# Grouped attention on one core: reordering the first loads, moving ScalarE's skip branch, and respacing the final range test

## The chip, the core and the metric

The kernel runs on one core of a Trainium2 chip. The core has five engines that run their own instruction streams and meet at semaphores: TensorE (PE, with its weight loads listed as PEld), VectorE (DVE), ScalarE (ACT), GpSimd (POOL) and SyncE (SP), which here issues every transfer. The metric is the device time of one execution in microseconds (us), lower is better. Three runs of the kernel before took 540.35, 540.84 and 541.56 us, median 540.84.

## The reference

The inputs are q (16 batches, 32 heads, 288 rows, 128 columns) and k and v (16 batches, 8 heads, 512 rows, 128 columns), all bf16 normals times 0.05. Four query heads share one key and value head.

```python
k = jnp.repeat(k, rep, axis=1)
v = jnp.repeat(v, rep, axis=1)
scale = D ** -0.5
scores = jnp.einsum("bhqd,bhkd->bhqk", q, k) * scale
p = _softmax(scores, axis=-1)
return jnp.einsum("bhqk,bhkd->bhqd", p, v)
```

## The kernel before

**Groups, slots, units.** A group is one key/value head of one batch with its 4 x 288 = 1152 query rows, which are 9 tiles of 128 rows. There are 128 groups, numbered g. The scores of one group, keys on the partitions, are 4 x 1152 = 4608 columns; they are cut into NC = 3 slots of 1536 columns, so there are 384 slots, numbered n. Four groups make a unit u; k and v are loaded by unit into NSLOT = 3 buffers, q by group into NQ = 12 buffers, and the output is stored by group from NO = 6 buffers.

**One slot.** PE computes the scores of slot n (`op_s`, L499) into one of two score buffers. ACT takes exp of them (`op_exp`, L537) with no maximum subtracted. PE multiplies with v, for the three row tiles of slot n - 4 (`op_pv`, L519; LAG = 4): 12 matmuls of 129 columns, where the 129th column of v is ones and gives the row sum. The output lies in one of two PSUM banks. DVE takes the reciprocals of the three row sums (`op_rc`, L554) and multiplies them into the output (`op_ev`, L565). In the text the product, the reciprocal and the multiplication of slot r are called pv(r), rc(r) and ev(r). POOL copies v to where the column of ones stands (`op_vc`, L547).

**What a step waits for.** The scores of slot n wait for k and q of the group and for the exp of slot n - 2. pv(r) waits for ev(r - 2), since it writes the same bank. ev(r) of a group g of 6 or more waits, on DVE and ahead of everything behind it there, until the store of group g - 6 has landed, since both use the same output buffer:

```python
waits = [("s_rc", r + 1)]
if g >= NO:
    waits.insert(0, ("s_o%d" % (g % NO), 16 * (g // NO)))
```

So ev(18), the first of group 6, waits for store 0; ev(24), the first of group 8, for store 2.

**SP's order.** SP issues all transfers in one stream: first the list `first` (k of groups 0 to 3 one by one, q of groups 0 to 3, v of groups 0 to 3), then the list `sp`, sorted by a due time written for each transfer (L600 to L611). k and q are transposing transfers (L432 and L453), v (L444) and the stores (L467, and L472 for the three pieces of the last group) are plain. Before the change the list opens with: q of groups 4, 5, 6, 7, then k of unit 1, q 8, v of unit 1, q 9, q 10, q 11, k of unit 2, v of unit 2, q 12, q 13, store 0, q 14, store 1, q 15, store 2, k of unit 3, v of unit 3, q 16, store 3.

**The fallback and the flag.** Since no maximum is subtracted, the kernel keeps a second, general program for inputs whose row sums leave a range. A flag chooses it at the end. DVE reduces all reciprocals to their largest and smallest (`op_stat`, L582 and L584, once per batch, and L669 and L671 over the batches) and compares them with the limits (`op_over`, L589 and L592). The reciprocals of the last ALONE = 15 row tiles (5 slots) are compared one by one, behind the last reciprocal. PE adds the comparisons over the partitions (L631), DVE adds the rest to one number (L674), and every engine loads it (L373) and branches on it (L377). SP, ahead of its branch, waits there until all stores have landed. All engines then drain and meet at a barrier (L329).

**Where the general code lies.** Each engine's instructions of the general program lie somewhere in its stream, and the function `general` makes it branch past them (L362). For POOL, DVE and SP this is near the top; for ACT it is between the last slot and the flag; for PE the code lies behind the end.

Of the kernel before, what the change touches and what calls it, by code (L numbers as in the profile page):

```python
# [287 lines left out]
def bass_standalone__gqa_softmax__near_ridge_kernel(  # L288
# [5 lines left out]
):  # L294
    B, Hq, Sq, D = q.shape
    _, Hkv, Sk, _ = k.shape
    P = 128
    R = (Hq // Hkv) * Sq
    NJ = Sk // P
    NT = R // P  # L300
    G = Hkv
    NG = B * G
    assert D == P and Sk % P == 0 and R % P == 0
    BANK = 512
    TPC = 3
    CH = TPC * BANK
    COLS = NJ * R
    NC = COLS // CH
# [3 lines left out]
    LAG = NC + 1  # L312
    UG = 4
    NU = NG // UG
    NSLOT = 3
    NQ = 12
    NPT = 3
    NO = 6
    NS = NG * NC
    LASTG = NG - 1  # L320
    ALONE = 5 * TPC


    q_v = q.rearrange("b h s d -> (b h s) d").rearrange("(x t) d -> x (t d)", t=NT)
# [4 lines left out]
    with ExitStack() as es:  # L329
# [29 lines left out]
        def general(eng, key, after):  # L359

            home[key] = nc.cur_bb
            eng.br(after + key)  # L362
            with nc.body("general_" + key):
                if key == "sp":
                    eng.sem_inc(sem["s_go"], 1)
                fns[key](eng)
                eng.br("done_" + key)
            nc.switch_bb(after + key)
# [25 lines left out]
        rl_sb = main.enter_context(nc.sbuf_tensor("rl_sb", [P, NG * NT], FP32))  # L394
        st_sb = main.enter_context(nc.sbuf_tensor("st_sb", [P, 2, B], FP32))
        ck_sb = main.enter_context(nc.sbuf_tensor("ck_sb", [P, 3], FP32))
        bad_sb = main.enter_context(nc.sbuf_tensor("bad_sb", [P, 2, ALONE + 1], FP32))
        one_f = main.enter_context(nc.sbuf_tensor("one_f", [P, 1], FP32))
# [6 lines left out]
        def need(eng, waits):  # L405

            left = []
            for (s, n) in waits:
                key = (id(eng), s)
                if seen.get(key, 0) < n:  # L410
                    seen[key] = n
                    left.append((sem[s], n))
            return left

        def emit(eng, waits, fn):
            waits = need(eng, waits)
            for (s, n) in waits[:-1]:
                eng.wait_ge(s, n)
            ins = fn()
            if waits:  # L420
                ins.wait_op(waits[-1][0], waits[-1][1], "sem-ge")
            return ins


        def op_k(u, gi=None):
            eng = nc.sync
            sl = u % NSLOT
            if u >= NSLOT:
                for (s, n) in need(eng, [("s_s", NC * UG * (u - NSLOT + 1))]):
                    eng.wait_ge(s, n)  # L430
            g0, g1 = (0, UG) if gi is None else (gi, gi + 1)
            eng.dma_start_transpose(  # L432
                kt_sb[:, sl, :, g0:g1].rearrange("d j g p -> d j (g p)"),
                k_v[(u * UG + g0) * P:(u * UG + g1) * P]
            ).then_inc(sem["us_k%d" % sl if gi is None else "s_k%d" % gi], 16)

        def op_v(u, gi=None):
            eng = nc.sync
            sl = u % NSLOT
            if u >= NSLOT:  # L440
                for (s, n) in need(eng, [("s_vc", UG * (u - NSLOT + 1))]):
                    eng.wait_ge(s, n)
            g0, g1 = (0, UG) if gi is None else (gi, gi + 1)
            eng.dma_start(  # L444
                vd_sb[:, sl, g0:g1], v_v[:, u * UG + g0:u * UG + g1]
            ).then_inc(sem["us_v%d" % sl if gi is None else "s_v%d" % gi], 16)

        def op_q(g):
            eng = nc.sync
            if g >= NQ:  # L450
                for (s, n) in need(eng, [("s_s", NC * (g - NQ + 1))]):
                    eng.wait_ge(s, n)
            eng.dma_start_transpose(qt_sb[:, g % NQ], q_v[g * P:(g + 1) * P]).then_inc(sem["s_q%d" % (g % NQ)], 16)  # L453
# [71 lines left out]
        def op_exp(n):  # L525
            eng = nc.scalar
            g, i = n // NC, n % NC
            waits = [("s_s", n + 1)]
            if g >= NPT:
                waits.insert(0, ("s_pv", NC * (g - NPT + 1)))  # L530
            if g == LASTG:
                w = TPC * P
                dst = pt_sb[:, g % NPT].rearrange("p (j r) -> p j r", r=R)[:, :, i * w:(i + 1) * w]
                src = ps_s[:, n % 2].rearrange("p (j r) -> p j r", r=w)
            else:
                dst, src = pt_sb[:, g % NPT, i * CH:(i + 1) * CH], ps_s[:, n % 2]
            emit(eng, waits, lambda: eng.activation(dst, src, ACTF.Exp, scale=scale)).then_inc(sem["s_e"], 1)  # L537
# [40 lines left out]
        def op_stat(b):  # L578
            eng = nc.vector
            w = G * NT  # L580
            a, e = b * w, (b + 1) * w - (ALONE if b == B - 1 else 0)
            emit(eng, [("s_rc", e // TPC)], lambda: eng.tensor_reduce(  # L582
                st_sb[:, 0, b:b + 1], rl_sb[:, a:e], AX.X, ALU.max))
            eng.tensor_reduce(st_sb[:, 1, b:b + 1], rl_sb[:, a:e], AX.X, ALU.min).then_inc(sem["s_stat"], 1)  # L584

        def op_over(hi, lo, x0, x1, wait, n):

            eng = nc.vector
            emit(eng, [wait], lambda: eng.tensor_scalar(  # L589
                out=bad_sb[:, 0, x0:x1], in0=hi, scalar1=SUM_MAX, scalar2=None, op0=ALU.is_gt)  # L590
            ).then_inc(sem["s_stat"], 1)
            emit(eng, [("s_stat", n)], lambda: eng.scalar_tensor_tensor(  # L592
                out=bad_sb[:, 1, x0:x1], in0=lo, scalar=1.0 / SUM_MAX, in1=bad_sb[:, 0, x0:x1],
                op0=ALU.is_lt, op1=ALU.add)).then_inc(sem["s_bad"], 1)
# [2 lines left out]
        first = [lambda: op_k(0, 0), lambda: op_q(0), lambda: op_k(0, 1), lambda: op_q(1), lambda: op_v(0, 0)]  # L597
        first += [lambda: op_k(0, 2), lambda: op_q(2), lambda: op_v(0, 1)]
        first += [lambda: op_k(0, 3), lambda: op_q(3), lambda: op_v(0, 2), lambda: op_v(0, 3)]
        sp = []  # L600
        for u in range(1, NU):
            t = -1.0 + u if u < NSLOT else NC * UG * (u - NSLOT + 1) + LAG
            sp.append((t, lambda u=u: op_k(u)))
            sp.append((t + 0.2, lambda u=u: op_v(u)))
        for g in range(UG, NG):
            sp.append((-0.9 + g / UG - 1.0 if g < NQ else NC * (g - NQ + 1) + 1.2, lambda g=g: op_q(g)))
        for g in range(LASTG):
            sp.append((NC * (g + 1) + LAG + 1.5, lambda g=g: op_store(g)))
        for i in range(NC):
# [3 lines left out]
        @block.sync  # L613
        def _(eng):
            for fn in first:
                fn()
            general(eng, "sp", "main_")
            for (_, fn) in sp:
                fn()
            choose(eng, "sp")  # L620

        @block.tensor
        def _(eng):
            for n in range(NS + LAG):
# [6 lines left out]
            emit(eng, [("s_ev", NS - 1), ("s_bad", 2)], lambda: eng.matmul(  # L631
                ps_o[0:1, NS % 2, 0:ALONE + 1], one_f[:], bad_sb[:, 1, :], start=True, stop=True)
            ).then_inc(sem["s_bad"], 1)
            choose(eng, "pe", behind=True)

        @block.scalar
        def _(eng):
            emit(eng, [("s_one", 1)], lambda: eng.activation(dum[:, 1:2], dum[:, 0:1], ACTF.Exp))  # L638
            for n in range(NS):
                op_exp(n)  # L640
            op_ev_last()
            general(eng, "act", "end_")
            choose(eng, "act")

        @block.gpsimd
# [7 lines left out]
        @block.vector  # L653
        def _(eng):
            eng.memset(dum[:], 0.0).then_inc(sem["s_one"], 1)  # L655
            eng.memset(one_f[:], 1.0)
            general(eng, "dve", "main_")
            per_b = G * NC
            for r in range(NS):
                op_rc(r)  # L660
                if r == NS - 1:
                    last = rl_sb[:, NG * NT - ALONE:NG * NT]
                    op_over(last, last, 0, ALONE, ("s_rc", NS), B + 3)
                op_ev(r)
                if r % per_b == per_b - 1 and r < NS - 1:
                    op_stat(r // per_b)
                if r == NS - 1 - ALONE // TPC:
                    op_stat(B - 1)
                    emit(eng, [("s_stat", B)], lambda: eng.tensor_reduce(  # L669
                        ck_sb[:, 0:1], st_sb[:, 0, :], AX.X, ALU.max))  # L670
                    eng.tensor_reduce(ck_sb[:, 1:2], st_sb[:, 1, :], AX.X, ALU.min).then_inc(sem["s_stat"], 1)  # L671
                    op_over(ck_sb[:, 0:1], ck_sb[:, 1:2], ALONE, ALONE + 1, ("s_stat", B + 1), B + 2)
            with nc.allow_low_precision(reason="a count of at most 2048"):
                emit(eng, [("s_bad", 3)], lambda: eng.tensor_reduce(  # L674
                    flag_i[:], ps_o[0:1, NS % 2, 0:ALONE + 1], AX.X, ALU.add)).then_inc(sem["s_flag"], 1)
            choose(eng, "dve")
# [30 lines left out]
```

## Time and profile before

| what | value |
|---|---|
| median of three runs | 540.84 us |
| the profiled execution | 541.11 us |
| its span in the profile | 539.4 us |
| outside the span | 1.71 us |
| PE busy in the span | 524.0 us (97%) |
| ACT busy | 522.1 us (97%) |
| DVE busy | 288.5 us (53%) |
| POOL busy | 73.8 us (14%) |
| transfers, mean | 204 GB/s, 110.08 MB |

The span is counted from the first instruction to the last one that the profile shows; times inside it are given from its start. A row of the timeline gives start, length, engine, line, operation, and in brackets how long the engine was idle before and for what. A row of the view of one line gives count, shortest, median and longest duration in ns, and first and last start. SP's rows are the issues of transfers; how long after the start of its issue a transfer has landed is a row of its own. The granted clock (PEclk) is the share of TensorE's full clock in a stretch.

### The profile page before, as it was taken

The numbers are of one execution on the slowest core, as the hardware profiler recorded it, in microseconds if no ns is written. First come the engines' busy times: TensorE is split into PE (matmuls) and PEld (weight loads), VectorE is DVE, ScalarE is ACT, GpSimd is POOL, SyncE is SP. The second block draws the span as 40 slices with busy tenths as digits, with TensorE's granted clock in tenths as the row PEclk, the third lists the DMA queues.
The fourth block names the chain that finished last, engine by engine and source line by source line (L and its number), as shares of the span: only waits on it lengthen the run. The fifth ranks groups of instructions, "written<-read, shape, count | busy, mean of one in ns | idle before, by whom it ended". The sixth has DMA issues, their size and how long they took to land.

```text
span 539.4 us, 14538 instructions
## 1 busy us (share of the span) xinstructions
PE 524.0 (97%) x6152; PEld 411.2 (76%) x6152; DVE 288.5 (53%) x809; ACT 522.1 (97%) x387; POOL 73.8 (14%) x133
## 2 busy tenths in 40 slices
PE   4799999999999999999999999999999999999997
PEld 1577777777777777777777777777777777777776
DVE  0445555555555555555555555555555555555555
ACT  5889999999999999999999999999999999999995
POOL 1021211100111101111101111101111101111000
PEclk9989999999999999999999999999999999999999
DMA  6999999999899988899998999989899988995212
GB/s 133 178 216 246 281 247 292 260 203 190 219 212 228 207 209 219 192 215 232 205 183 220 219 215 233 211 186 199 224 220 225 219 182 216 204 224 154 87 67 92
DMA packets 253944, 110.08 MB, mean 204 GB/s; under 512 B 220848, under 2 KB 237616, under 8 KB 253872
## 3 DMA queue, kind: packets, MB, share of 16 engines
q1 hardware_dynamic: 253872, 109.08, 90.2%
q8 instruction: 50, 0.82, 0.6%
q14 instruction: 22, 0.18, 0.1%
HBM read 16.78 MB, written 37.75 MB: 101 GB/s over the span
## 4 chain that ended last, share of the span: by engine, by line
PE 94%; ACT 3%; DVE 1%; DMA 1%; issue 1%; SPq 0%
PE ps_o L519 49%; PE ps_s L499 45%; ACT pt_sb L537 3%; DMA qt_sb<-in_q_dram 1%; DVE o_sb L565 0%; SPq L432 0%; DVE rl_sb L554 0%; DVE bad_sb L589 0%; DVE bad_sb L592 0%; DVE ck_sb L669 0%; DVE st_sb L584 0%; DVE flag_i L674 0%; DVE st_sb L582 0%; DVE ck_sb L671 0%
## 5 line engine op out<-in xcount | busy, mean ns | idle before, releaser
L537 ACT ACTIVATE pt_sb<-ps_s 128x1536 bf16<-128x1536 f32 x384 | 520.2, 1452 | 10.6 <-PE ps_s L499 10.6
L519 PEld LDWEIGHTS ps_o<-v_sb,pt_sb 128*128 128x128 bf16 x4596 | 300.2, 98 | 55.0 <-DVE o_sb L565 0.6
L519 PE MATMUL ps_o<-v_sb,pt_sb 128*128 128x129 bf16 x4596 | 332.6, 221 | 0.4 <-DVE o_sb L565 0.4
L499 PE MATMUL ps_s<-qt_sb,kt_sb 128*128 128x512 bf16 (+3 forms) x1542 | 313.8, 326 | 11.6 <-DMA qt_sb<-in_q_dram 6.7
L565 DVE TENSOR_TENSOR o_sb<-ps_o,rl_sb 128x384 bf16<-128x384 f32 x383 | 213.6, 558 | 13.5 <-DVE rl_sb L554 0.3
L554 DVE RECIPROCAL rl_sb<-ps_o 128x3 f32<-128x3 f32 x383 | 69.3, 181 | 233.9 <-PE ps_o L519 233.9
L499 PEld LDWEIGHTS ps_s<-qt_sb,kt_sb 128*128 128x128 bf16 x1542 | 130.2, 98 | 69.5 <-DMA qt_sb<-in_q_dram 6.7
L547 POOL COPY v_sb<-vd_sb 128x512 bf16<-128x512 bf16 x128 | 73.3, 616 | 421.3 <-DMA vd_sb<-in_v_dram 392.5
L584 DVE TENSOR_REDUCE st_sb<-rl_sb 128x1 f32<-128x72 f32 (+1 forms) x16 | 3.5, 217 | 0.0
L582 DVE TENSOR_REDUCE st_sb<-rl_sb 128x1 f32<-128x72 f32 (+1 forms) x16 | 3.5, 217 | 0.0
L573 ACT ACTIVATE o_sb<-ps_s,rl_sb 128x128 bf16<-128x128 f32 x1 | 0.4, 368 | 2.9 <-DVE rl_sb L554 2.9
L638 ACT ACT_TABLE_LOAD x1 | 1.3, 1283 | 0.8 <-PEq L692 0.8
L631 PE MATMUL ps_o<-bad_sb,one_f 128*1 128x16 f32 x2 | 0.2, 176 | 0.7 <-DVE bad_sb L592 0.7
L519 PE MATMUL ps_s<-v_sb,pt_sb 128*128 128x129 bf16 x12 | 0.9, 221 | 0.0
L631 PEld LDWEIGHTS ps_o<-bad_sb,one_f 128*1 128x1 f32 x2 | 0.1, 80 | 0.9 <-DVE bad_sb L592 0.9
L519 PEld LDWEIGHTS ps_s<-v_sb,pt_sb 128*128 128x128 bf16 x12 | 0.7, 98 | 0.0
L655 DVE MEMSET dum<- 128x2 f32 x1 | 0.1, 60 | 0.9 <-PEq L692 0.9
L565 DVE TENSOR_TENSOR o_sb<-ps_s,rl_sb 128x256 bf16<-128x256 f32 x1 | 0.4, 418 | 0.0
L647 POOL MEMSET v_sb<- 128x48 bf16 x1 | 0.3, 311 | 0.3 <-POOLq L692 0.3
L638 ACT ACTIVATE dum<-dum 128x1 f32<-128x1 f32 x1 | 0.2, 203 | 0.0
L592 DVE SCALAR_TENSOR_TENSOR bad_sb<-rl_sb,bad_sb 128x15 f32<-128x15 f32 x1 | 0.2, 175 | 0.0
L589 DVE TENSOR_SCALAR bad_sb<-rl_sb 128x15 f32<-128x15 f32 x1 | 0.2, 174 | 0.0
(11 smaller groups left out, 1.4 us busy)
## 6 DMA issues: line engine op xcount, KB each, us to landing
out_dram<-o_sb SPq DMA_DIRECT2D x127, 288.0 KB, 3.4
vd_sb<-in_v_dram SPq DMA_DIRECT2D x31, 512.0 KB, 5.1
qt_sb<-in_q_dram SPq DMA_TRANSPOSE x128, 4.6
kt_sb<-in_k_dram SPq DMA_TRANSPOSE x35, 4.7
vd_sb<-in_v_dram SPq DMA_DIRECT2D x4, 128.0 KB, 2.9
out_dram<-o_sb SPq DMA_DIRECT2D x3, 96.0 KB, 1.8
```

The costliest lines, as they stand in the source:

```text
L499: ins = emit(eng, waits if x == 0 else [], lambda: eng.matmul(ps_s[:, n % 2, c:c + w], kt_sb[:, sl, j, gi, :], qg[:, r0:r0 + w], start=Tru ...
L519: ins = emit(eng, waits if a == 0 and j == 0 else [], lambda: eng.matmul(outs(r)[:, a, :], pt_sb[:, g % NPT, j * R + t * P:j * R + (t + 1) ...
L537: emit(eng, waits, lambda: eng.activation(dst, src, ACTF.Exp, scale=scale)).then_inc(sem["s_e"], 1)
L547: emit(eng, waits, lambda: eng.tensor_copy(v_sb[:, sl, gi * NJ:(gi + 1) * NJ, 0:D], vd_sb[:, sl, gi].rearrange("p (j d) -> p j d", d=D))). ...
L554: emit(eng, [("s_pv", r + 1)], lambda: eng.reciprocal(rl_sb[:, TPC * r:TPC * (r + 1)].unsqueeze(2), outs(r)[:, :, D:DV])).then_inc(sem["s_ ...
L565: emit(eng, waits, lambda: eng.tensor_tensor(out=o_sb[:, g % NO, t0:t0 + n, :], in0=outs(r)[:, 0:n, 0:D], in1=rl_sb[:, TPC * r:TPC * r + n ...
L573: emit(eng, [("s_o%d" % (LASTG % NO), 16 * (LASTG // NO)), ("s_rc", NS)], lambda: eng.activation(o_sb[:, LASTG % NO, NT - 1, :], outs(NS - ...
L582: emit(eng, [("s_rc", e // TPC)], lambda: eng.tensor_reduce(st_sb[:, 0, b:b + 1], rl_sb[:, a:e], AX.X, ALU.max))
L584: eng.tensor_reduce(st_sb[:, 1, b:b + 1], rl_sb[:, a:e], AX.X, ALU.min).then_inc(sem["s_stat"], 1)
L631: emit(eng, [("s_ev", NS - 1), ("s_bad", 2)], lambda: eng.matmul(ps_o[0:1, NS % 2, 0:ALONE + 1], one_f[:], bad_sb[:, 1, :], start=True, st ...
L638: emit(eng, [("s_one", 1)], lambda: eng.activation(dum[:, 1:2], dum[:, 0:1], ACTF.Exp))
L647: eng.memset(v_sb[:, :, :, D:DV], 1.0)
```

## The change

It has three parts.

1. In SP's list the transfers ahead of the first slots are reordered: k of unit 1, q 4, q 5, v of unit 1, q 6, q 7, k of unit 2, q 8, q 9, v of unit 2, q 10, q 11, then q 12, q 13, store 0 as before. From unit 3 on, k is due at the first slot of a unit plus 0.5 where it was due 4 slots later, and v stays due 4 slots behind it. After store 0 the list reads q 14, store 1, k of unit 3, q 15, store 2, v of unit 3, q 16, store 3.
2. ACT branches past its general code right behind its first small activation, and not behind its last one.
3. ALONE becomes 24 (8 slots). The reductions over the batches and their comparison, which followed one another behind ev(378), stand behind ev(375), ev(376) and ev(377). The comparison of the last 24 reciprocals, which stood between rc(383) and ev(383), stands behind ev(383).

```diff
-    ALONE = 5 * TPC
+    ALONE = 8 * TPC
...
         for u in range(1, NU):
-            t = -1.0 + u if u < NSLOT else NC * UG * (u - NSLOT + 1) + LAG
-            sp.append((t, lambda u=u: op_k(u)))
-            sp.append((t + 0.2, lambda u=u: op_v(u)))
+            t = NC * UG * (u - NSLOT + 1) if u >= NSLOT else -2 * NC * UG + u
+            sp.append((t + 0.5, lambda u=u: op_k(u)))
+            sp.append((t + (LAG if u >= NSLOT else 0.65), lambda u=u: op_v(u)))
         for g in range(UG, NG):
-            sp.append((-0.9 + g / UG - 1.0 if g < NQ else NC * (g - NQ + 1) + 1.2, lambda g=g: op_q(g)))
+            t = NC * (g - NQ + 1) + 1.2 if g >= NQ else -2 * NC * UG + g // UG + 0.51 + 0.1 * (g % UG)
+            sp.append((t, lambda g=g: op_q(g)))
...
             emit(eng, [("s_one", 1)], lambda: eng.activation(dum[:, 1:2], dum[:, 0:1], ACTF.Exp))
+            general(eng, "act", "main_")
             for n in range(NS):
                 op_exp(n)
             op_ev_last()
-            general(eng, "act", "end_")
             choose(eng, "act")
...
             per_b = G * NC
+            w0 = NS - 1 - ALONE // TPC
+            last = rl_sb[:, NG * NT - ALONE:NG * NT]
             for r in range(NS):
                 op_rc(r)
-                if r == NS - 1:
-                    last = rl_sb[:, NG * NT - ALONE:NG * NT]
-                    op_over(last, last, 0, ALONE, ("s_rc", NS), B + 3)
                 op_ev(r)
                 if r % per_b == per_b - 1 and r < NS - 1:
                     op_stat(r // per_b)
-                if r == NS - 1 - ALONE // TPC:
+                if r == w0:
                     op_stat(B - 1)
+                if r == w0 + 1:
                     emit(eng, [("s_stat", B)], lambda: eng.tensor_reduce(
                         ck_sb[:, 0:1], st_sb[:, 0, :], AX.X, ALU.max))
                     eng.tensor_reduce(ck_sb[:, 1:2], st_sb[:, 1, :], AX.X, ALU.min).then_inc(sem["s_stat"], 1)
+                if r == w0 + 2:
                     op_over(ck_sb[:, 0:1], ck_sb[:, 1:2], ALONE, ALONE + 1, ("s_stat", B + 1), B + 2)
+            op_over(last, last, 0, ALONE, ("s_rc", NS), B + 3)
```

## The prediction

> **What bounds the kernel now.** The page first, for the size of things; then ScalarE's timeline over the whole span, because a kernel with two engines at 97% loses time only where both stop.
>
> ```profile
> span 539.4 us, 14538 instructions
> DMA  6999999999899988899998999989899988995212
> out_dram<-o_sb SPq DMA_DIRECT2D x127, 288.0 KB, 3.4
> kt_sb<-in_k_dram SPq DMA_TRANSPOSE x35, 4.7
> ```
>
> ```profile
> 8.18 16.22 ACT L537 ACTIVATE pt_sb<-ps_s 128x1536 bf16<-128x1536 f32 x12 [5.88 <-PE ps_s L499]
> 28.46 1.45 ACT L537 ACTIVATE pt_sb<-ps_s 128x1536 bf16<-128x1536 f32 x1 [4.06 <-PE ps_s L499]
> 30.62 502.54 ACT L537 ACTIVATE pt_sb<-ps_s 128x1536 bf16<-128x1536 f32 x371 [0.71 <-PE ps_s L499]
> 536.01 0.37 ACT L573 ACTIVATE o_sb<-ps_s,rl_sb 128x128 bf16<-128x128 f32 x1 [2.85 <-DVE rl_sb L554]
> ```
>
> From 30.62 us on, 371 exps run without a gap at 502.54 / 371 = 1.355 us each: the pace of a slot. No part of the change touches that pace. What it can touch is the hole between the 12th and 14th exp (4.06 + 0.71 us) and the tail behind the last exp. PE's timeline and the stretches around the hole show what it is:
>
> ```profile
> 22.50 0.87 PE L519 MATMUL ps_o<-v_sb,pt_sb 128*128 128x129 bf16 x12
> 26.99 1.44 PE L499 MATMUL ps_s<-qt_sb,kt_sb 128*128 128x512 bf16 x4 [3.63 <-issue]
> ```
>
> ```profile
> 23.40:26.60 3.20, 0.00 (x0) 0.00 (x0) 0.74 (x2) 1.00 (x1) 0.00 (x0) 1.00 1.03 203
> 26.60:30.00 3.40, 3.01 (x18) 2.04 (x19) 0.20 (x2) 1.45 (x1) 0.00 (x0) 0.50 1.17 235
> ```
>
> PE runs pv(7) at 22.50 and then stands idle for 3.63 us until the scores of slot 12, the first of unit 1. When it resumes its granted clock (third number from the end) is 0.50 until about 30.0. What it waited for is in SP's timeline:
>
> ```profile
> 14.36 7.66 SPq L453 DMA_TRANSPOSE qt_sb<-in_q_dram  x4
> 22.05 2.15 SPq L432 DMA_TRANSPOSE kt_sb<-in_k_dram  x1
> 25.86 0.58 SPq L444 DMA_DIRECT2D vd_sb<-in_v_dram  x1
> 40.01 0.58 SPq L467 DMA_DIRECT2D out_dram<-o_sb  x1
> 44.07 0.57 SPq L467 DMA_DIRECT2D out_dram<-o_sb  x1
> 44.68 2.69 SPq L432 DMA_TRANSPOSE kt_sb<-in_k_dram  x1
> ```
>
> k of unit 1 is issued at 22.05, behind four q transfers that are needed later; with the median 4.7 us to landing it is there at 26.75, and PE starts at 26.99. That is the stall part 1 aims at.
>
> **Part 1, the hole, and where the stall goes.** In the new order k of unit 1 is issued at 14.36 and q 4 behind it. The scores of slot 12 would want them about 0.7 us behind the start of pv(7), at 23.2. k issued at 14.36 lands near 14.36 + 4.7 = 19.1; q 4 follows at the pace 7.66 / 4 = 1.92 us of an issue, near 21. Both are in time, so this wait goes. The next transfers too: q 5 and v 1 follow within some 5 us and are wanted three slots (4.1 us) and four slots later.
>
> What is late next? The stores. The row of the multiplications up to ev(18), the issue-to-landing of store 0, and two rows of the timeline there:
>
> ```profile
> L565 DVE TENSOR_TENSOR o_sb<-ps_o,rl_sb x19: 557/558/559, 14.1 to 43.7; 128x384 bf16<-128x384 f32 x19
> ```
>
> ```profile
> L467 SPq DMA_DIRECT2D out_dram<-o_sb x1: 580/580/580, 40.0 to 40.0; - x1
> DMA to landing us min/median/max: 3.2/3.2/3.2
> ```
>
> ```profile
> 43.74 0.56 DVE L565 TENSOR_TENSOR o_sb<-ps_o,rl_sb 128x384 bf16<-128x384 f32 x1
> 45.32 0.87 PE L519 MATMUL ps_o<-v_sb,pt_sb 128*128 128x129 bf16 x12
> ```
>
> The 19th multiplication, ev(18), starts at 43.74, and it may not start before store 0 has landed: 40.01 + 3.2 = 43.2. So today it clears that wait by only 0.5 us. Store 0 stands behind the same fourteen transfers in both orders (q 4 to q 13, k and v of units 1 and 2), and the DMA row of the page is at nine tenths from its second slice on, so the reordering gives no reason for store 0 to land earlier. I keep 43.2.
>
> Without any stall pv(20) would start at 22.50 + 13 x 1.355 = 40.1; today it starts at 45.32, so the hole costs 5.2 us in all: 3.63 idle and 1.6 for the restart at half clock. After the change ev(18) starts at 43.25, ends 0.56 later, and pv(20), which waits for it, starts about 43.87. That is 45.32 - 43.87 = 1.45 us earlier than now, not 5.2. Behind the waiting ev(18) on DVE stand rc(19) and ev(19); behind pv(20) on PE stand the scores of slot 25 and so ACT's exp. PE's last work before the stop is the scores of slot 24, ending near 40.2, so PE is idle 3.6 us, as long as now, only 17 us later.
>
> The clock then decides how much of the 1.45 is kept. From the windows above: after 3.2 us without a matmul the clock fell to 0.50 and stayed there 3.4 us, at a cost of 1.6. The bounds for the new stop are 0 (the clock stays) and 1.6. I take the middle, 0.8, since the row shows the fall once for a stop of this length and nothing shows what it would be at another moment. Part 1 at the start: 1.45 - 0.8 = **0.65 us gained**, bounds -0.15 and 1.45.
>
> The Trainium skill, "TensorE: Matmul & The Clock Gate", Part 1, says that the clock halves after at least one idle window of about 3.4 us, and that the windows run freely and don't start with the kernel. By that rule a stop of 3.6 us holds a whole window only if one happens to begin in the first 0.2 us of it, an estimate of 6 in 100; the sum would be 539.2 us by it. The trace speaks for less than a whole idle window being enough, as the fall came at 26.6, 3.24 us after the last matmul.
>
> k of unit 3 moves ahead of q 15 and store 2. Its issue takes 2.69 us, so store 2, issued at 44.07 now and landed by 47.5 with the median 3.4, lands at 50.2 or, if all of that k transfer must be served before it, up to about 51.5. ev(24) needs it; with pv(20) at 43.87 + 0.8 the product behind it, pv(26), falls at 44.67 + 6 x 1.355 = 52.8, so store 2 may land as late as 52.1 (0.56 for ev(24), some 0.1 for its semaphores). Nothing, then, with 0.6 us to spare at worst. Later units have k ahead of one more q and store in the queue, but the full 371-exp run shows that no wait decides there. Without that cover the same 2.7 us per unit would count.
>
> **Part 2 and part 3, the tail.** The rows behind the last exp, and the last steps of each engine (views of single lines):
>
> ```profile
> 531.51 1.57 PE L519 MATMUL ps_o<-v_sb,pt_sb 128*128 128x129 bf16 x24
> 532.65 0.17 DVE L554 RECIPROCAL rl_sb<-ps_o 128x3 f32<-128x3 f32 x1
> 533.47 1.58 PE L519 MATMUL ps_o<-v_sb,pt_sb 128*128 128x129 bf16 x24 [0.39 <-DVE o_sb L565]
> 536.01 0.17 DVE L589 TENSOR_SCALAR bad_sb<-rl_sb 128x15 f32<-128x15 f32 x1
> 536.31 0.42 DVE L565 TENSOR_TENSOR o_sb<-ps_s,rl_sb 128x256 bf16<-128x256 f32 x1
> 536.69 0.16 DVE L674 TENSOR_REDUCE flag_i<-ps_o 1x1 int32<-1x16 f32 x1
> ```
>
> ```profile
> L362 ACTq COMPARE_BRANCH  x1: 33/33/33, 536.0 to 536.0; - x1
> L373 DVEq TENSOR_LOAD <-flag_i x1: 542/542/542, 536.9 to 536.9; - x1
> L373 ACTq TENSOR_LOAD <-flag_i x1: 463/463/463, 538.6 to 538.6; - x1
> L329 DVEq DRAIN  x1: 134/134/134, 538.4 to 538.4; - x1
> L329 SPq DRAIN  x1: 136/136/136, 539.0 to 539.0; - x1
> L329 ACTq DRAIN  x1: 8/8/8, 539.1 to 539.1; - x1
> L472 SPq DMA_DIRECT2D out_dram<-o_sb x1: 333/333/333, 536.8 to 536.8; - x1
> DMA to landing us min/median/max: 1.8/1.8/1.8
> ```
>
> Two engines end last, together. SP waits for the last store (536.76 + 1.8 = 538.55) and drains at 539.0 to 539.16. ACT branches past its general code at 536.0, can load the flag only at 538.6, 1.7 us behind DVE, and drains at 539.1. Only both together make the end earlier.
>
> ACT: at the top the same branch costs up to 538.6 - 536.0 = 2.6 us from about 1 us on, and ACT has nothing to do until 8.18 (5.88 idle): hidden. Without that cover it would be 2.6 us. At the end ACT then loads the flag when DVE does, and it ends like DVE, whose drain starts 0.9 us behind its load's end. If ACT's own last branch took the 2.6 us of this one, it would end at 537.0 + 0.46 + 2.6 = 540.1, 0.9 later than now; three engines (POOL, DVE, SP) already have the new layout and two of them show their drains before ACT's, so I take DVE's 0.9.
>
> Stores: the reductions leave slot 378, where they held rc(379) to 532.65 and PE for 0.39. The first 12 of the 24 matmuls at 531.51 are done 0.87 later, so rc(379) can start at 532.41, 0.24 earlier, and everything behind it with it. In slots 375 to 377 each piece (0.25 to 0.4 us by the same rows' spacing) fits DVE's idle 1.355 - 0.77 = 0.58 us a slot. At the very end ev(383) starts where the comparison starts now: 536.31 - 536.01 = 0.30 earlier. The last store is issued 0.24 + 0.30 = 0.54 earlier, and SP's drain ends at 538.62.
>
> Flag: the two comparisons now follow ev(383) and end 0.3 later against rc(383), which is 0.24 earlier; 24 columns for 15 add nothing I can see at 0.17 us for 15. The flag comes 0.1 us later, and DVE's drain ends at 538.58 + 0.1 = 538.68. The end moves from 539.16 to 538.68, **0.5 us gained**; bounds 0.54 and, with ACT's slow last branch, -0.9.
>
> **Sum.** Against the profiled execution's own time, 541.11 us (span 539.4, 1.71 around it; 0.27 above the median of 540.84 and inside the runs' 540.35 to 541.56): 541.11 - 0.65 - 0.5 = 539.96, **540.0 us**, 0.84 below the median.
>
> **Rivals.**
>
> *The clock holds.* The stop moves to ev(18) but PE restarts at full clock: 541.11 - 1.45 - 0.5 = 539.2. For it: the fall depends on when in the idle time it is decided. Against: the same length of stop brought it down once.
>
> *The hole closes altogether.* Store 0 would have to land by about 39.4 (pv(20) at 40.1 less 0.65), before SP even issues it now. Gain 5.2 + 0.5: 535.4. For it: k ahead of q might let transfers flow better, and the hole did look like a k wait alone; against: the same bytes stand ahead of store 0.
>
> *Slower: store 2 behind k of unit 3.* Here is that k transfer's landing now:
>
> ```profile
> L432 SPq DMA_TRANSPOSE kt_sb<-in_k_dram x1: 2692/2692/2692, 44.7 to 44.7; - x1
> DMA to landing us min/median/max: 7.0/7.0/7.0
> ```
>
> If all its 7.0 us come ahead of store 2, this lands at 47.5 + 7.0 = 54.5, ev(24) ends 55.1, and pv(26) starts at 55.2 where it now starts at 45.32 + 6 x 1.355 = 53.45: 1.75 lost, 0.5 gained, and a second restart at half clock adds up to 1.6: 542.4 without, about 543 with half of it. It decides from a landing at 53.3 on, where the tail's 0.5 is used up. Against it: part of the 7.0 is queueing that store 2 has today too.
>
> *No net effect.* The stop moves, the clock falls for its full 1.6 (0.15 lost), and some third engine holds the tail: 541.0.
>
> **How the numbers follow.** What a measurement of this kernel tells from no change is about 0.2%, 1.08 us: below 539.76 is faster, above 541.92 slower. Forecast (540.0, own range 539.2 to 541.0) 0.45; clock holds 0.22; hole closes 0.07; slower by store 2 0.11; no net effect 0.15. Faster: a third of the forecast's range (0.16) with the clock rival (0.20 of its 0.22) and the closed hole, 0.43. Slower 0.11. Same, the rest, 0.46. Store 0's landing is not known better than about an issue (1 us) either way; the range of 8 in 10 is 538.3 to 541.6, which leaves out the closed hole and the slow rival.
>
> **What would show it.** Right: k of unit 1 issued near 14.4, no idle time on PE near 23; ev(18) starting within 0.1 us of store 0's landing, with PE idle some 3 to 4 us ahead of pv(20) and the clock low behind it or not; ACT's flag load beside DVE's; DVE and SP draining last, near together. Wrong: store 0 landing well before 43 (closed hole), a second stop of PE ahead of pv(26) (store 2), ACT's first exp later than 8.2 (its branch or code loading in the way at the top), or ACT draining last.

## The result, and the profile after

The changed kernel takes 541.2 us (median of four runs, 539.79 to 541.70), the kernel before 541.2 us over its runs beside it; the ratio is 0.9997 with a 95% interval of 0.9972 to 1.0022. No change can be told. The profiled execution of the changed kernel took 541.70 us, with a span of 540.0.

The time did move inside the span. First ScalarE's timeline of the changed kernel (start, length, engine, line, operation; idle time before it in brackets), to be held against the four rows of before:

```profile
8.43 2.79 ACT L537 ACTIVATE pt_sb<-ps_s 128x1536 bf16<-128x1536 f32 x2 [6.13 <-PE ps_s L499]
11.43 31.00 ACT L537 ACTIVATE pt_sb<-ps_s 128x1536 bf16<-128x1536 f32 x23 [0.21 <-PE ps_s L499]
46.39 1.45 ACT L537 ACTIVATE pt_sb<-ps_s 128x1536 bf16<-128x1536 f32 x1 [3.95 <-PE ps_s L499]
48.97 1.45 ACT L537 ACTIVATE pt_sb<-ps_s 128x1536 bf16<-128x1536 f32 x1 [1.13 <-PE ps_s L499]
50.62 483.58 ACT L537 ACTIVATE pt_sb<-ps_s 128x1536 bf16<-128x1536 f32 x357 [0.20 <-PE ps_s L499]
```

The hole ahead of the 13th exp is gone: 23 exps run from 11.43 to 42.43 without a gap. A hole of the same size has opened ahead of the 26th, 3.95 + 1.13 + 0.20 us where it was 4.06 + 0.71. The long run behind it keeps its pace, 483.58 / 357 = 1.355 us.

What opened it is in the waits (who waited for what: us in total, how many times, the longest), and in VectorE's and TensorE's timelines:

```profile
DVE o_sb L565 <- DMA out_dram<-o_sb: 5.1, 1, 5.1
```

```profile
38.88 0.18 DVE L554 RECIPROCAL rl_sb<-ps_o 128x3 f32<-128x3 f32 x1 [0.58 <-PE ps_o L519]
44.11 0.56 DVE L565 TENSOR_TENSOR o_sb<-ps_o,rl_sb 128x384 bf16<-128x384 f32 x1 [5.05 <-DMA out_dram<-o_sb]
```

```profile
40.03 0.81 PE L499 MATMUL ps_s<-qt_sb,kt_sb 128*128 128x512 bf16 x4
44.73 0.88 PE L519 MATMUL ps_o<-v_sb,pt_sb 128*128 128x129 bf16 x12 [3.88 <-DVE o_sb L565]
46.14 1.51 PE L519 MATMUL ps_o<-v_sb,pt_sb 128*128 128x129 bf16 x12
```

The waiting multiplication at 44.11 is ev(18): it stands 5.05 us on a transfer out, the first store. PE stops behind the scores of slot 24 and takes up pv(20) 3.88 us later. SP's timeline and the landing of that store say when it came:

```profile
14.48 2.57 SPq L432 DMA_TRANSPOSE kt_sb<-in_k_dram  x1
39.03 0.58 SPq L467 DMA_DIRECT2D out_dram<-o_sb  x1
41.68 3.62 SPq L432 DMA_TRANSPOSE kt_sb<-in_k_dram  x1
46.75 0.58 SPq L467 DMA_DIRECT2D out_dram<-o_sb  x1
```

```profile
L467 SPq DMA_DIRECT2D out_dram<-o_sb x1: 578/578/578, 39.0 to 39.0; - x1
DMA to landing us min/median/max: 5.0/5.0/5.0
```

k of unit 1 is issued at 14.48 and is in time. Store 0 is issued 1 us earlier than before (39.03 for 40.01), needs 5.0 us for 3.2, and lands at 44.0, later than the 43.2 of before. ev(18) starts 0.1 us behind it. The clock fell again, but not at once: from 44.7 to 46.0 us, with PE at work, it was granted at 1.00. The stretch from 46 us on (the granted clock is the third number from the end):

```profile
46.00:49.50 3.50, 3.50 (x26) 2.64 (x24) 1.15 (x3) 1.98 (x2) 0.00 (x0) 0.51 1.06 241
```

At the end, ACT's flag load now stands beside the others, and DVE drains last (views of single lines):

```profile
L373 ACTq TENSOR_LOAD <-flag_i x1: 468/468/468, 538.0 to 538.0; - x1
L373 DVEq TENSOR_LOAD <-flag_i x1: 546/546/546, 538.1 to 538.1; - x1
...
L329 ACTq DRAIN  x1: 8/8/8, 538.6 to 538.6; - x1
L329 SPq DRAIN  x1: 136/136/136, 539.3 to 539.3; - x1
L329 DVEq DRAIN  x1: 134/134/134, 539.6 to 539.6; - x1
```

The last exp ends at 50.62 + 483.58 = 534.2, so the tail is 540.0 - 534.2 = 5.8 us. Before it was 539.4 - (30.62 + 502.54) = 6.2. In what follows "the tail" is this stretch, from the end of the last exp to the end of the span.

### The profile page after: what moved, and what is told of

The parts are those of the page before. It is cut to its first block, busy times and chain, and to the rows that moved or that the text cites. A ratio compares the mean times of both kernels' runs of the same rounds, so it can differ in the third digit from the quotient of the medians.

```text
span 540.0 us, 14438 instructions
## 1 busy us (share of the span) xinstructions
PE 519.7 (96%) x6052; PEld 411.6 (76%) x6152; DVE 288.3 (53%) x809; ACT 522.1 (97%) x387; POOL 74.0 (14%) x133
## 4 chain that ended last, share of the span: by engine, by line
PE 95%; DMA 2%; issue 1%; DVE 1%; ACT 1%; SPq 0%; DVEq 0%
PE ps_o L519 50%; PE ps_s L499 44%; DMA out_dram<-o_sb 1%; DMA qt_sb<-in_q_dram 1%; ACT pt_sb L537 1%; DVE o_sb L565 0%; SPq L432 0%; SPq L453 0%; DVE rl_sb L554 0%; PE ps_o L633 0%; DVE bad_sb L592 0%; DVE flag_i L678 0%; DVE bad_sb L589 0%; DVEq L418 0%
## 5 line engine op out<-in xcount | busy, mean ns | idle before, releaser
L499 PE MATMUL ps_s<-qt_sb,kt_sb 128*128 128x512 bf16 (+3 forms) x1442 | 297.2, 323 | 11.7 <-DMA qt_sb<-in_q_dram 6.9
```

The costliest lines, as they stand in the source:

```text
L499: ins = emit(eng, waits if x == 0 else [], lambda: eng.matmul(ps_s[:, n % 2, c:c + w], kt_sb[:, sl, j, gi, :], qg[:, r0:r0 + w], start=Tru ...
```

## The experiments

The theory to test: part 1 removes the wait for k of unit 1, and what it frees is held back by the wait of ev(18) for store 0. The rivals: another part of the change opened the second hole; the transfers at the start are too slow as a whole, so that some transfer is late in any case; the hole is a fixed price.

**One part at a time.** The old order with parts 2 and 3, and the new order alone. Both diffs are against the changed kernel and cut to their core.

```diff
 e1_tail_only
-            t = NC * UG * (u - NSLOT + 1) if u >= NSLOT else -2 * NC * UG + u
+            t = -1.0 + u if u < NSLOT else NC * UG * (u - NSLOT + 1) + LAG
...
-            t = NC * (g - NQ + 1) + 1.2 if g >= NQ else -2 * NC * UG + g // UG + 0.51 + 0.1 * (g % UG)
+            sp.append((-0.9 + g / UG - 1.0 if g < NQ else NC * (g - NQ + 1) + 1.2, lambda g=g: op_q(g)))
 e2_order_only
-    ALONE = 8 * TPC
+    ALONE = 5 * TPC
...
-            general(eng, "act", "main_")
...
+            general(eng, "act", "end_")
...
-            op_over(last, last, 0, ALONE, ("s_rc", NS), B + 3)
```

> The kernel before with parts 2 and 3 of the change and the old order of loads. Theory (the stop moved from k of unit 1 to store 0, the tail is a gain of its own): the hole stays ahead of slot 12, 3.6 us of PE idle with the half clock or without; from the start of the last exp to the end of the span 6.2 us at most 5.8 (about 0.45 less than before); time 0.45 below before, so between 540.4 and 541.1, inside the noise. Rival (the tail edits do nothing): the stretch from the last exp to the end stays 6.2.

> The kernel before with part 1 of the change alone. Theory: no idle time ahead of slot 12, ev(18) within 0.15 us of the landing of store 0 (43 to 44.5), PE idle 3 to 4 us ahead of pv(20), time 541 to 542, not faster than before; the last exp to the end 6.2 us as before. Rival (the stop comes from the branch of ACT or the flag edits): no stop at ev(18) here, and the time falls to about 536.

The expectation of the first counts its 6.2 and 5.8 us from the start of the last exp; they are the tail as defined above, from its end. Measured: 540.44 us, ratio 0.9984 (0.9963 to 1.0004), with the hole where it was before and a tail of 5.8:

```profile
8.31 16.36 ACT L537 ACTIVATE pt_sb<-ps_s 128x1536 bf16<-128x1536 f32 x12 [6.01 <-PE ps_s L499]
28.47 1.45 ACT L537 ACTIVATE pt_sb<-ps_s 128x1536 bf16<-128x1536 f32 x1 [3.80 <-PE ps_s L499]
31.05 502.71 ACT L537 ACTIVATE pt_sb<-ps_s 128x1536 bf16<-128x1536 f32 x371 [1.13 <-remote]
```

The order alone: 540.66 us, ratio 0.9993 (0.9966 to 1.0020), a tail of 6.2, and the hole at the 26th exp. Its waits:

```profile
DVE o_sb L565 <- DMA out_dram<-o_sb: 5.4, 1, 5.4
PEld ps_o L519 <- DVE o_sb L565: 5.1, 2, 4.5
PE ps_o L519 <- DVE o_sb L565: 4.6, 2, 4.2
```

So the second hole belongs to part 1 and the tail to parts 2 and 3. The time of 541 to 542 expected for the order alone was missed by 0.3 us.

**More output buffers, under both orders.** o_sb has NO buffers; with 8, ev(24) is the first that waits for a store.

```diff
 e3_after_8_out (the changed kernel), e4_before_8_out (the kernel before)
-    NO = 6
+    NO = 8
```

> The changed kernel with 8 output buffers for 6, so that store 0 is waited for by ev(24) and not by ev(18). Theory (the store wait alone holds the gain back): ev(24) would run at 46.6 without a stop and store 0 lands at 43 to 44, so no stop of PE over 1 us behind the first scores, the clock stays, time 5.2 + 0.45 below before: 535.5, from 535 to 536.2. Rival (the transfers as a whole are too slow at the start, and the next one is late in the place of store 0): a new stop of some us between 38 and 60 us, time 538 to 541.

> The kernel before with 8 output buffers and no other edit. Theory (before, the stop is k of unit 1, and the store wait is cleared by 0.5 us): the hole ahead of slot 12 stays at 3.6 us of PE idle, time 540.3 to 541.7, same as before. Rival (the store wait costs before as well): 1 us or more faster.

With the new order: 536.09 us (535.64 to 536.17), ratio 0.9898 (0.9862 to 0.9933). ScalarE's timeline has no hole left:

```profile
8.47 2.79 ACT L537 ACTIVATE pt_sb<-ps_s 128x1536 bf16<-128x1536 f32 x2 [6.17 <-PE ps_s L499]
11.42 517.10 ACT L537 ACTIVATE pt_sb<-ps_s 128x1536 bf16<-128x1536 f32 x382 [0.16 <-PE ps_s L499]
```

With the old order: 541.64 us, ratio 0.9992 (0.9973 to 1.0011), the hole ahead of slot 12 as before. Either edit alone gives nothing, both together 5.1 us (541.2 less 536.09). The rival of too slow transfers falls: with room for the output no transfer makes an exp wait behind the second one.

**One and two buffers fewer.**

```diff
 e9_after_7_out, e5_after_5_out (the changed kernel)
-    NO = 6
+    NO = 7      (e9)
+    NO = 5      (e5)
```

> The changed kernel with 7 output buffers: ev(21) waits for store 0, ev(24) for store 1, ev(30) for store 3. Theory: ev(21) would run at 43.15 and its product has about 0.8 us to spare, store 0 lands at 43 to 44; store 3 lands at 54 to 56 and ev(30) would run at 55.3: stops of together 0 to 1.5 us, all too short for the clock to fall; time 536.1 to 537.6. Rival (a fixed price as long as fewer than 8 buffers make anything wait): 541.

> The changed kernel with 5 output buffers for 6: now ev(15) waits for store 0. Theory (time follows the landing of store 0 minus the slot that needs it): ev(15) would run at 35.0, store 0 lands at 43 to 44, so pv(17) starts at about 44.6 where it would start at 36.6: 8 us lost, and 1.6 for the half clock; time three slots (4.06 us) above the changed kernel: 545.5, from 544.3 to 546.5. Rival (the stop is a fixed price of the early transfers, whoever waits for them): 541 to 542.

Seven buffers: 536.04 us, ratio 0.9903 (0.9886 to 0.9919). ev(21) waits 1.0 us for store 0, but that fits what its product has to spare:

```profile
DVE o_sb L565 <- DMA out_dram<-o_sb: 1.3, 2, 1.0
```

```profile
11.45 517.09 ACT L537 ACTIVATE pt_sb<-ps_s 128x1536 bf16<-128x1536 f32 x382 [0.21 <-PE ps_s L499]
```

Five buffers: 544.70 us, ratio 1.0062 (1.0045 to 1.0078), with a wait of 7.4 us:

```profile
DVE o_sb L565 <- DMA out_dram<-o_sb: 7.4, 1, 7.4
```

One buffer fewer is three slots, 4.06 us; measured were 544.70 - 541.2 = 3.5. Two amounts that were not expected meet in this. Store 0 landed earlier in this profile (ev(15) starts at 42.41, where ev(18) started at 44.11), which leaves 4.06 - 1.70 = 2.4. The rest, about 1.1, is the restart, which cost that much more than with six buffers: the granted clock was 0.50 from 43.0 to 46.4 and still 0.64 on average from 46.4 to 49.8, and its mean over the execution was 0.993 or 0.994 in all four runs, for 0.996 or 0.997 in the three slower runs of the changed kernel. Here the half clock lasted about twice as long as the 3.4 us behind the other stops. The price follows the slot that needs the store, so it isn't fixed.

**Store 0 earlier, six buffers.**

```diff
 e6_store0_early (the changed kernel)
-            sp.append((NC * (g + 1) + LAG + 1.5, lambda g=g: op_store(g)))
+            sp.append((-2 * NC * UG + 2.7 if g == 0 else NC * (g + 1) + LAG + 1.5, lambda g=g: op_store(g)))
```

> The changed kernel, 6 output buffers, with store 0 issued ahead of q 10 instead of behind q 13; nothing else is moved. Theory: store 0 lands near 36 and ev(18) runs at 39.1 without a stop; then store 1 is late (lands 45.6, ev(21) would run at 43.15: 1.6 us with its 0.8 to spare), and stores 2 and 3 by another 0.5 to 2 us; the stops are short, the clock stays; time 537.5 to 540. Rival (no store is late once store 0 is not): 536. Rival (transfers are too slow on the whole, moving one only exchanges which is late by as much): 541.

Measured 539.0 us (538.16 to 539.95), ratio 0.9963 (0.9945 to 0.9981). ScalarE's timeline has two short holes, and the waits count three for a store:

```profile
11.08 35.03 ACT L537 ACTIVATE pt_sb<-ps_s 128x1536 bf16<-128x1536 f32 x26 [0.18 <-PE ps_s L499]
47.32 4.16 ACT L537 ACTIVATE pt_sb<-ps_s 128x1536 bf16<-128x1536 f32 x3 [1.20 <-PE ps_s L499]
52.55 478.17 ACT L537 ACTIVATE pt_sb<-ps_s 128x1536 bf16<-128x1536 f32 x353 [1.07 <-PE ps_s L499]
```

```profile
DVE o_sb L565 <- DMA out_dram<-o_sb: 5.2, 3, 2.4
```

As expected stores 1, 2 and 3 are late next: DVE waits 2.4, 2.2 and 0.7 us for them, and PE stops for 1.2 and 1.0 us. Moving one store gives part of the gain; the buffers give all of it.

**The tail's two parts.**

```diff
 e7_branch_only (the kernel before)
+            general(eng, "act", "main_")
             for n in range(NS):
                 op_exp(n)
             op_ev_last()
-            general(eng, "act", "end_")
 e8_flag_only (the kernel before)
-    ALONE = 5 * TPC
+    ALONE = 8 * TPC
...
-                if r == NS - 1:
-                    last = rl_sb[:, NG * NT - ALONE:NG * NT]
-                    op_over(last, last, 0, ALONE, ("s_rc", NS), B + 3)
...
+            op_over(last, last, 0, ALONE, ("s_rc", NS), B + 3)
```

> The kernel before with part 2 alone (ACT passes its general code at the top). One look, for the tail: the stretch from the end of the last exp to the end of the span, which is 6.2 us before and 5.8 with parts 2 and 3. Theory (only both parts together make the end earlier, since SP behind the last store ends with ACT): ACT's flag load moves from 1.7 us behind DVE's to beside it, SP drains last, the stretch stays 6.1 to 6.3. Rival (the branch was the whole of the tail's gain): 5.8.

> The kernel before with part 3 alone (flag comparisons spread and behind ev(383)). One look, for the tail: the stretch from the end of the last exp to the end of the span. Theory: the last store is issued about 0.5 us earlier after the last exp (3.1 us behind its end for 3.6), but ACT loads the flag 2.5 us behind its branch as before and drains last, 0.24 earlier at most: the stretch is 5.9 to 6.2. Rival (the store alone sets the end): 5.7.

The branch alone: ACT drains at 537.1, SP last at 538.5, a tail of 6.0 (the last exp ends at 532.84, the span at 538.85), a little less than expected. The flag edits alone: ACT loads the flag at 539.1, about 1.5 us behind DVE (537.6), and drains last; a tail of 6.2 (533.70 to 539.94), at the upper edge of what was expected. Together 5.8. Their single times, 540.57 and 541.72 us, say nothing of the whole at these differences.

**The order and the buffers without parts 2 and 3.**

```diff
 e10_order_8_out (e2_order_only)
-    NO = 6
+    NO = 8
```

> The kernel before with part 1 and 8 output buffers, without parts 2 and 3: the two edits that did nothing alone, together. Theory: no stop of PE over 0.9 us behind slot 3; the tail from the end of the last exp to the end of the span is 6.2 us again (5.8 to 5.9 with parts 2 and 3); the first scores start at 6.6 to 6.75, as in the kernels whose ACT does not branch at the top (6.8 to 7.0 in most that do); time 536.2 to 536.8. Rival (part 2 or 3 is needed for the gain at the start): 540 or more.

Measured 536.12 us, ratio 0.9919 (0.9905 to 0.9934), a hair below what was expected. Its timeline:

```profile
7.88 2.79 ACT L537 ACTIVATE pt_sb<-ps_s 128x1536 bf16<-128x1536 f32 x2 [5.58 <-PE ps_s L499]
10.88 517.09 ACT L537 ACTIVATE pt_sb<-ps_s 128x1536 bf16<-128x1536 f32 x382 [0.21 <-PE ps_s L499]
```

The tail is 534.35 - 527.97 = 6.4 us (the span with its second decimal), 0.5 longer than with parts 2 and 3 in e3 (534.39 - 528.52 = 5.9), and the first exp comes 0.6 us earlier (7.88 for 8.47). The two nearly cancel: parts 2 and 3 give nothing that can be told here.

## Why the prediction was right, and where it was off

The forecast was 540.0 us, no change that can be told, with a range of 538.3 to 541.6; measured were 541.2, so the 0.84 us that the forecast lay below the median before did not come. That no change would be told was a near thing on the prediction's own chances, 0.46 against 0.43 for faster: the mechanism was foreseen, the verdict less so.

**The wait removed, and where it went: right, and shown.** k of unit 1 is issued at 14.48 (forecast near 14.4), the stop ahead of slot 12 is gone, and the new stop is at ev(18), 0.1 us behind the landing of store 0. e3 and e9 show that this wait alone held the gain: without it the same order is 1% faster. e4 shows that before the change the store wait cost nothing yet.

**The size of the first term: wrong, by two amounts.** The prediction had 0.65 us gained at the start; the profiled run lost 1.04 (the exp of slot 27 starts at 50.62, before at 49.58).
- "I keep 43.2" for the landing of store 0: it landed at 44.0. The step from "the same fourteen transfers" to the same landing was too exact; in the profiles here with the new order and store 0 behind q 13 it landed between 42.3 and 44.0. pv(20) started at 44.73 for the predicted 43.87, 0.86 us.
- "I take the middle, 0.8" for the clock: the profile shows the full price. pv(20) is 45.32 - 44.73 = 0.59 earlier than before, and the exps behind it 1.04 later, so 1.63 went into the restart. That is another 0.83.

These two and 0.06 in the tail are the difference between the predicted -1.15 and the measured 541.70 - 541.11 = +0.59 of the profiled runs. This accounts for these two executions only; the four runs of the changed kernel differ by more than that among themselves.

**The rival "the clock holds": not the likeliest, but it happens, before the change too.** Each run has its mean granted clock; 3.4 us at half clock take 0.003 off it (half of 3.4 / 540). Of 45 runs of the kernel before that were taken beside the experiments, 11 have 0.999 or more, with a median of 539.73 us, and 34 have 0.997 or less, with a median of 541.60. (Three of these have 0.994, as in e5, and took 542.46 to 543.10.) Of the four runs of the changed kernel one has 0.999 (539.79), three 0.996 or 0.997 (median 541.63). At the same clock the two kernels take the same time, as far as one run and three can tell. That the stop stands in the runs at 0.999 too and only the fall is missing is inferred: all eight profiles with a stop of PE of 2.98 us or more show the fall, and the four without such a stop show none. The flaw was to charge the fall in full to the profiled run of before and by half to the forecast. The stops are about as long, 3.6 and 3.9 us, and nothing here shows another chance of a fall for one than for the other; without the fall on either side, the prediction's own numbers give 40.1 + 3.63 = 43.7 for pv(20) before and 43.87 after, a gain of nothing.

**Store 2 behind k of unit 3: right that it doesn't decide.** That k transfer took 3.62 us to issue where I had 2.69, store 2 was issued at 46.75 and landed 3.4 us later, at the 50.2 that the prediction gave first, and no second long stop follows; the slow rival fell. The 51.5 given as its latest landing is worked out from no row, and the rival's own price has 54.5 for the same case.

**The tail: right.** 0.44 us gained for 0.5 forecast, from 6.2 to 5.8. That it takes both parts is shown roughly, by one profile each: alone the branch gave 0.2 and the flag edits nothing. DVE drains last, 5.55 us behind the last exp (its drain ends at 539.75, less 534.20) where the prediction had 538.68 - 533.16 = 5.52.

**What hides the branch at the top: not quite.** I costed it at nothing since ACT idles until 8.18. The first exp came at 8.43 in the changed kernel, and an exp later than 8.2 was among the prediction's own signs of being wrong. In the seven profiles with the branch at the top the first scores start at 6.62 to 6.97, on average 6.85; in the five without, at 6.38 to 6.74, on average 6.61. That is some 0.2 us lost at the start on average, which in the changed kernel disappears in the wait for store 0. The two ranges overlap, so that the branch is the cause is not shown, and why it should delay the first scores was not tried.

## What to carry to other kernels

When a wait is removed, look for the next wait that the freed work will run into, and compare when its releaser comes with when the work will now want it: here 0.5 us of slack behind a 5 us stall told the result. A load that comes earlier helps only if the buffers at the other end let the work run ahead; 7 output buffers for 6 turned an edit worth nothing into 1%. Where a stop brings the clock down in some runs and not in others, price the fall alike on both sides of the comparison.

## What the runs showed of the hardware that was not expected

A stop of less than 3 us was enough for the clock to fall. In e7 PE stopped for 2.98 us only, and the clock fell to 0.50 just after it had resumed (TensorE's timeline, and two stretches):

```profile
26.46 1.38 PE L499 MATMUL ps_s<-qt_sb,kt_sb 128*128 128x512 bf16 x4 [2.98 <-issue]
```

```profile
23.48:26.46 2.98, 0.00 (x1) 0.03 (x1) 0.74 (x2) 1.04 (x1) 0.00 (x0) 1.00 1.10 243
26.55:29.90 3.35, 3.35 (x19) 2.29 (x20) 0.69 (x2) 1.45 (x1) 0.00 (x0) 0.50 1.06 220
```

The Trainium skill, "TensorE: Matmul & The Clock Gate", Part 1, puts the fall behind at least one idle window of about 3.4 us; here 2.98 us sufficed, so the measurement decides. The stops of 1.2 and 1.0 us in e6 left the clock at 1.00.

Nor does the fall come at a fixed time after the last matmul, as the 3.24 us in the prediction may suggest. It came 3.1 us after it in e7 (26.55 less 23.48), and 5.2 us after it in the changed kernel (46.0 less 40.84), where PE had been at work again for 1.3 us. What sets the moment is not shown here.

With six buffers and the new order, SP's issue of one and the same kind of transfer took from 2.57 us (k of unit 1) to 3.62 us (k of unit 3), and what stands behind it on SP is issued that much later (q 15 at 45.34, behind 41.68 + 3.62 = 45.30). What makes an issue long was not tried.
